# Turning attention weights on VectorE and through DRAM in place of TensorE transposes

## The chip, the cores and the metric

One core of one Trainium2 chip. The metric is the time of the program on the device in microseconds (us). Each time below is the median of some executions of one kernel; figures from a profile are those of one profiled execution. All executions quoted here fell in the fast state, within 1.5% of the fastest of the same kernel. The "granted clock" is TensorE's, as a share of full speed. A matmul of fp32 data leaves two records in the trace, a transpose one. "PE" is TensorE's matmul pipe, "DVE" VectorE, "ACT" ScalarE, "POOL" GpSimd, and "SPq" the sequencer that issues the DMAs.

## The reference

Eight batches of eight heads, 576 positions, 64 values per head. Attention keeps only scores within `tau` of the row's maximum; a feed-forward block with ELU follows. All of it is fp32.

```python
scores = scale * np.matmul(q, k.transpose(0, 1, 3, 2))       # (8, 8, 576, 576)
thresh = np.max(scores, axis=-1, keepdims=True) - tau
scores = np.where(scores >= thresh, scores, -1000000000.0)
attn = np.exp(scores - np.max(scores, axis=-1, keepdims=True))
attn = attn / (np.sum(attn, axis=-1, keepdims=True) + 1e-09)
x = merge_heads(np.matmul(attn, v))                           # (4608, 512)
h = x @ w_in                                                  # (4608, 2048)
g = np.where(h > 0.0, h, np.exp(np.minimum(h, 0.0)) - 1.0)
out = g @ w_out                                               # (4608, 512)
```

## The kernel before

Heads are worked on in 32 pairs, four pairs to a batch. A pair has five steps: four of 128 query positions and a tail step for the last 64 positions of both heads. In a step, `begin` multiplies scores and takes maxima and exponentials, `finish` forms the kept and normalised weights `w`, and one step later `turn` turns `w`, because the product with `v` needs the key position on the partition axis. When two steps (part a) or the last three (part b) of a pair are turned, `values` multiplies.

```python
def finish(pr, i, hs):
    ...
    for h in hs:                                   # DVE: w = (sc >= th) * e, sum beside it
        nc.vector.scalar_tensor_tensor(w[:, h], sc[:, :, :HALF], st["th"][:, h : h + 1], e, ALU.is_ge, ALU.mult, ...)
    ...
    for h in hs:                                   # POOL: w = w / sum
        nc.gpsimd.tensor_scalar(w[:, h], w[:, h], rs[:, h : h + 1], 1.0, ALU.mult, ALU.mult)

def turn(pr, i):
    w = open_steps.pop((pr, i))["w"].rearrange("p h a n -> p (h a n)")
    ...
    for h in range(2):
        rt = ps_t.tile([P, NC, P], FP32, name="rt", tag="rt")
        for c in range(NC):                        # PE: 128x128 transposes into PSUM
            k0 = h * (S + TAIL) + c * P
            transpose(rt[:, c], w[:, k0 : k0 + P])
        nc.scalar.copy(wT[:, h * NC : (h + 1) * NC, cs], rt)     # ACT: PSUM to SBUF
    ...                                            # one more for the last 64 keys of both heads

# the loop from the second batch on; the feed-forward work of the batch before fills TensorE
for n in range(per_seq, len(steps) + 2):
    if n < len(steps):
        ahead(*steps[n])                           # turns q and k, loads two pairs ahead
        begin(*steps[n], [0, 1] if steps[n][1] < NC else [0])
        ...
        finish(*steps[n], [0, 1] if steps[n][1] < NC else [0])
    if n - 1 < len(steps):
        turn(*steps[n - 1])
    behind(*steps[n - 2])                          # values, two steps behind
    due = min(due + rate, len(units))
    while due >= 1 and units:                      # 1.7 units of four matmuls per step
        f, a = units.popleft(); f(*a); due -= 1
```

The order in this loop is not the order on the chip: the compiler schedules each engine's instructions within the dependencies.

## Time and profile before

| | before |
|---|---|
| time, median of 4 in the comparison with the changed kernel | 1615.38 us (1613.23 to 1628.98) |
| period of a group (four pairs and one batch of feed-forward work) | 178.6 us |
| PE busy, whole run | 97% |
| mean granted clock | 0.989 |

The lines on which the prediction rests are shown in the prediction.

### The profile page before, as it was taken

The numbers are of one execution on the slowest core, as the hardware profiler recorded it, in microseconds if no ns is written. First come the engines' busy times: TensorE is split into PE (matmuls) and PEld (weight loads), VectorE is DVE, ScalarE is ACT, GpSimd is POOL, SyncE is SP. The second block draws the span as 40 slices with busy tenths as digits, with TensorE's granted clock in tenths as the row PEclk, the third lists the DMA queues.
The fourth block names the chain that finished last, engine by engine and source line by source line (L and its number), as shares of the span: only waits on it lengthen the run. The fifth ranks groups of instructions, "written<-read, shape, count | busy, mean of one in ns | idle before, by whom it ended". The sixth has DMA issues, their size and how long they took to land.

```text
span 1611.8 us, 17586 instructions
## 1 busy us (share of the span) xinstructions
PE 1570.4 (97%) x5952; PEld 786.4 (49%) x5952; DVE 735.0 (46%) x1670; ACT 586.1 (36%) x1109; POOL 379.6 (24%) x779
## 2 busy tenths in 40 slices
PE   7899889999999999999999999999999999999998
PEld 4554444554454445544555544554555454444443
DVE  6778773455335543455335543455345533220210
ACT  4665653343334433344334433344234333110110
POOL 4654552221222212222122212212122222000000
PEclk8999999999999999999999999999999999999999
DMA  5334541111111101110111011111110000000000
GB/s 108 69 81 104 142 130 36 32 19 23 29 29 29 23 15 36 36 23 15 30 35 30 15 25 27 34 23 23 28 34 10 9 7 14 7 1 20 7 7 20
DMA packets 200553, 55.68 MB, mean 35 GB/s; under 512 B 191760, under 2 KB 191760, under 8 KB 200464
## 3 DMA queue, kind: packets, MB, share of 16 engines
q1 hardware_dynamic: 200464, 54.56, 15.2%
q8 instruction: 48, 0.79, 0.2%
q14 instruction: 41, 0.34, 0.1%
HBM read 45.09 MB, written 9.44 MB: 34 GB/s over the span
## 4 chain that ended last, share of the span: by engine, by line
PE 82%; DVE 7%; POOL 4%; ACT 2%; issue 2%; DMA 1%; SPq 1%; POOLq 0%; DVEq 0%; ACTq 0%
PE po L299 30%; PE ph L285 26%; PE sc L197 9%; PE rt L221 8%; PE pv L269 8%; DVE w L213 3%; POOL w L218 2%; PE pv L266 2%; DVE mx L199 1%; ACT e L204 1%; POOL wtop L134 1%; DMA wst<-in_moe_w_out_dram 1%; DVE gt L290 1%; ACT fe L287 1%; DVE fe L288 1%
## 5 line engine op out<-in xcount | busy, mean ns | idle before, releaser
L299 PE MATMUL po<-w_out_sb,gt 128*128 128x512 f32 x1152 | 520.0, 597 | 0.0
L285 PE MATMUL ph<-xt,w_in_sb 128*128 128x512 f32 x1024 | 464.1, 597 | 0.0
L199 DVE TENSOR_REDUCE mx<-sc 128x1 f32<-128x576 f32 x288 | 207.4, 751 | 304.7 <-PE sc L197 304.6
L299 PEld LDWEIGHTS po<-w_out_sb,gt 128*128 128x128 f32 x1152 | 209.7, 191 | 236.5 <-issue 236.0
L218 POOL TENSOR_SCALAR w<-w,rs 128x576 f32<-128x576 f32 x288 | 217.0, 763 | 357.3 <-DVE rs L216 326.8
L213 DVE SCALAR_TENSOR_TENSOR w<-sc,th,e 128x576 f32<-128x576 f32 x288 | 226.5, 815 | 158.5 <-ACT e L204 150.8
L285 PEld LDWEIGHTS ph<-xt,w_in_sb 128*128 128x128 f32 x1024 | 184.7, 190 | 204.0 <-issue 203.0
L204 ACT ACTIVATE e<-sc,nb,keep 128x576 f32<-128x576 f32 x288 | 227.4, 829 | 83.8 <-POOL nb L200 83.5
L221 PE MATMUL rt<-ident,w 128*128 128x128 f32 (+1 forms) x1344 | 211.5, 284 | 17.9 <-POOL w L218 12.0
L221 PEld LDWEIGHTS rt<-ident,w 128*128 128x128 f32 (+1 forms) x1344 | 153.4, 143 | 118.5 <-issue 46.1
L197 PE MATMUL sc<-kT,qT 64*128 64x288 f32 x1024 | 192.9, 439 | 16.6 <-DVE kT L172 8.2
L288 DVE TENSOR_SCALAR fe<-fe 128x512 f32<-128x512 f32 x144 | 63.7, 443 | 315.3 <-ACT fe L287 315.3
L287 ACT ACTIVATE fe<-ph 128x512 f32<-128x512 f32 x144 | 85.9, 596 | 287.8 <-PE ph L285 287.8
L197 PEld LDWEIGHTS sc<-kT,qT 64*128 64x128 f32 x1024 | 107.1, 190 | 127.1 <-issue 84.9
L200 POOL TENSOR_SCALAR nb<-mx,nkeep 128x2 f32<-128x2 f32 (+1 forms) x176 | 52.1, 296 | 480.8 <-DVE mx L199 404.9
L238 ACT COPY wTa<-rt 128x512 f32<-128x512 f32 x128 | 70.9, 587 | 163.1 <-PE rt L221 161.1
L238 ACT COPY wTb<-rt 128x512 f32<-128x512 f32 x128 | 72.2, 584 | 129.3 <-PE rt L221 128.1
L290 DVE SCALAR_TENSOR_TENSOR gt<-ph,fe 128x512 f32<-128x512 f32 x144 | 99.4, 690 | 5.8
L304 ACT COPY ot<-po 128x512 f32<-128x512 f32 x36 | 21.1, 585 | 181.4 <-PE po L299 181.4
L269 PE MATMUL pv<-wTb,vm 128*64 128x320 f32 x512 | 76.0, 439 | 0.0
L269 PE MATMUL pv<-wTa,vm 128*64 128x256 f32 x512 | 63.6, 391 | 0.0
L285 PE MATMUL ph<-xtail,w_in_sb 128*128 128x512 f32 x128 | 55.1, 592 | 0.0
(45 smaller groups left out, 666.7 us busy)
## 6 DMA issues: line engine op xcount, KB each, us to landing
qm<-in_q_dram SPq DMA_DIRECT2D x128, 72.0 KB, 2.6
km<-in_k_dram SPq DMA_DIRECT2D x128, 72.0 KB, 2.5
vm<-in_v_dram SPq DMA_DIRECT2D x64, 128.0 KB, 2.4
wst<-in_moe_w_in_dram SPq DMA_DIRECT2D x16, 512.0 KB, 4.0
wst<-in_moe_w_out_dram SPq DMA_DIRECT2D x16, 512.0 KB, 3.8
out_dram<-ot SPq DMA_DIRECT2D x32, 256.0 KB, 2.0
vd<-in_v_dram SPq DMA_DIRECT2D x64, 16.0 KB, 2.1
out_dram<-ot SPq DMA_DIRECT2D x8, 128.0 KB, 2.3
```

The lines of the kernel that those rows point to most:

```text
L197: nc.tensor.matmul(scs[h][:, a, :HALF], qs[r], kT[r, k0 : k0 + HALF], start=True, stop=True)
L199: nc.vector.tensor_reduce(st["mx"][:, h : h + 1], scs[h][:, :, :HALF], axis=AX.XY, op=ALU.max)
L204: nc.scalar.activation(e, scs[h][:, :, :HALF], AF.Exp, bias=st["nb"][:, h : h + 1], scale=keep)
L213: nc.vector.scalar_tensor_tensor(w[:, h], sc[:, :, :HALF], st["th"][:, h : h + 1], e, ALU.is_ge, ALU.mult, accum_out=sm[:, h : h + 1])
L218: nc.gpsimd.tensor_scalar(w[:, h], w[:, h], rs[:, h : h + 1], 1.0, ALU.mult, ALU.mult)
L221: nc.tensor.matmul(dst, src, ident, is_transpose=True, skip_group_check=True)
L238: nc.scalar.copy(wT[:, h * NC : (h + 1) * NC, cs], rt)
L269: nc.tensor.matmul(pv[h * D : (h + 1) * D, :n], vm[:, h, c], wT[:, h * NC + c], start=False, stop=(c == NC - 1), skip_group_check=True)
L285: nc.tensor.matmul(ph, w_in_sb[:, j, ft * P : (ft + 1) * P], xt[:, j], start=(j == 0), stop=(j == KJ - 1))
L287: nc.scalar.activation(e, ph, AF.Exp)
L290: nc.vector.scalar_tensor_tensor(gt, ph, 0.0, e, ALU.max, ALU.add)
L299: nc.tensor.matmul(po[:, :DM], gts[ft][:, it * P : (it + 1) * P], w_out_sb[:, ft], start=(ft == 0), stop=(ft == NFT - 1))
```

## The change

From the eighth pair on (25 of 32 pairs, 125 steps), DVE turns `w` in 32x32 squares inside each partition quarter. The squares must still change quarters: four DMAs write the result to DRAM and one reads it back in the right order. TensorE loses 42 transposes per pair, ScalarE the copies behind them.

```diff
+    SWITCH = NPAIR + 3
...
+        if pr >= SWITCH:
+            x = late["x"].tile([P, NT * 2 * GK], FP32, name="x")
+            nc.vector.transpose(x, w)
+            there = dram.tile([NT, T, NT, 2 * GK], FP32, name="there")
+            for p in range(NT):
+                nc.sync.dma_start(there[:, :, p].rearrange("c k n -> k c n"),
+                                  x[p * T : (p + 1) * T].rearrange("k (c n) -> k c n", c=NT))
+            back = there.rearrange("c k p n -> (c k) p n")
+            if i < NC:
+                nc.sync.dma_start(wT[:, g0 : g0 + NT].rearrange("p g c n -> p g (c n)"), back)
+            else: ...                              # the tail step's two outer parts of wTb
+            return
...
-    for n in range(per_seq, len(steps) + 2):
+    for n in range(per_seq, len(steps) + 3):
...
-        behind(*steps[n - 2])
+            turned.append(steps[n - 1])
+        if len(turned) > (2 if late and n < len(steps) else 1) or n >= len(steps):
+            behind(*turned.popleft())              # values three steps behind
```

Cut here: a new layout of `w` and `wT` (keys in another order, so `v` is loaded in 16 small pieces per pair in place of 4), two memsets of `w` in a tail step, products of part b with 384 columns in place of 320 for the first of them, loads one step later, and weight staging buffers that are given back at the switch.

More of the change, by code (lines that the diff above doesn't have):

```diff
@@ L38 @@
     HALF = S // 2
+    T = 32
+    NT = P // T
+    GK = S // NT
+    NCH = 2 * NC + 1
     KJ = DM // P
@@ L44 @@
     FAR = 3.0e37
-    T = 32
+    SWITCH = NPAIR + 3
     assert (D, DM, TAIL * 2, B * TAIL, KJ) == (64, H * D, P, MAIN, NPAIR)
@@ L54 @@
     xpool = ctx.enter_context(tc.tile_pool(name="xpool", bufs=2))
-    wstage = ctx.enter_context(tc.tile_pool(name="wstage", bufs=2))
     gpool = ctx.enter_context(tc.tile_pool(name="gpool", bufs=NFT + 1))
     epool = ctx.enter_context(tc.tile_pool(name="epool", bufs=2))
+    dram = ctx.enter_context(tc.tile_pool(name="dram", bufs=4, space=bass.MemoryType.DRAM))
+    early = ExitStack()
+    wstage = early.enter_context(tc.tile_pool(name="wstage", bufs=2))
+    late = {}
     ps_t = ctx.enter_context(tc.tile_pool(name="ps_t", bufs=2, space=PSUM))
@@ L129, in convert_w @@
         nc.vector.scalar_tensor_tensor(top, hi, 0xC0000000, top, ALU.bitwise_and, ALU.bitwise_or)
-        rest = wstage.tile([P, WN], I32, name="wrest", bufs=1)
+        rest = lo.bitcast(I32)
         nc.scalar.mul(rest, lo, 2.0**-29)
@@ L158, in load @@
         vd = vds[pr % NVD]
+        if SWITCH <= pr < SWITCH + NVD:
+            nc.gpsimd.memset(vd, 0.0)
         for i in range(2):
-            vh = v[b, 2 * j + i]
-            nc.sync.dma_start(vm[:, i], vh[:MAIN].rearrange("(c p) d -> p c d", p=P))
-            r = slice(i * TAIL, (i + 1) * TAIL)
-            nc.sync.dma_start(vd[r, r], vh[MAIN:])
+            if pr < SWITCH:
+                r = slice(i * TAIL, (i + 1) * TAIL)
+                nc.sync.dma_start(vm[:, i], v[b, 2 * j + i, :MAIN].rearrange("(c p) d -> p c d", p=P))
+                nc.sync.dma_start(vd[r, r], v[b, 2 * j + i, MAIN:])
+                continue
+            for g in range(NT):
+                vg = v[b, 2 * j + i, g * GK : (g + 1) * GK]
+                m0, x0, r0 = (0, P, T * g) if i == 0 else (GK - P, 0, T * g + GK - P)
+                nc.sync.dma_start(vm[T * g : T * (g + 1), i], vg[m0 : m0 + P].rearrange("(c t) d -> t c d", t=T))
+                nc.sync.dma_start(vd[r0 : r0 + GK - P, i * D : (i + 1) * D], vg[x0 : x0 + GK - P])
         raws[pr] = *tiles, vm, vd
@@ L172, in prep @@
             nc.vector.transpose(dst, src.rearrange("p j d -> p (j d)"))
-        nc.gpsimd.tensor_copy(kT[D:, :TAIL], kT[D:, S:])
+        if pr < SWITCH:
+            nc.gpsimd.tensor_copy(kT[D:, :TAIL], kT[D:, S:])
         qd = qds[pr % NQD]
@@ L186, in begin @@
             open_steps[pr, i] = {
-                "w": att.tile([P, 2, 2, HALF], FP32, name="w"),
+                "w": att.tile([P, 2 * S], FP32, name="w"),
                 **{x: small.tile([P, 2], FP32, name=x) for x in ("mx", "nb", "th", "sm", "rs")},
@@ L194, in begin @@
             for h in hs:
-                k0 = a * HALF + (0 if h else TAIL)
+                k0 = a * HALF + (0 if h and pr < SWITCH else TAIL)
                 r, qs = (slice(h * D, (h + 1) * D), qT[:, i * P : (i + 1) * P]) if i < NC else (slice(0, P), qd)
@@ L210, in finish @@
         w, sm, rs = st["w"], st["sm"], st["rs"]
+        wg = w.rearrange("p (a g h n) -> p a g h n", a=2, h=2, n=GK)
+        if pr < SWITCH:
+            parts = [(slice(0, P), h, w[:, h * S : (h + 1) * S].rearrange("p (a g n) -> p a g n", a=2, n=GK)) for h in hs]
+        elif i < NC:
+            parts = [(slice(0, P), h, wg[:, :, :, h]) for h in hs]
+        else:
+            parts = [(slice(h * TAIL, (h + 1) * TAIL), 0, wg[h * TAIL : (h + 1) * TAIL, :, :, h]) for h in range(2)]
+            for h in range(2):
+                nc.gpsimd.memset(wg[h * TAIL : (h + 1) * TAIL, :, :, 1 - h], 0.0)
+        for r, s, wv in parts:
+            sc, e = st[s]
+            sc = sc[r, :, :HALF].rearrange("p a (g n) -> p a g n", n=GK)
+            nc.vector.scalar_tensor_tensor(wv, sc, st["th"][r, s : s + 1], e[r].rearrange("p a (g n) -> p a g n", n=GK),
+                                           ALU.is_ge, ALU.mult, accum_out=sm[r, s : s + 1])
         for h in hs:
-            sc, e = st.pop(h)
-            nc.vector.scalar_tensor_tensor(w[:, h], sc[:, :, :HALF], st["th"][:, h : h + 1], e, ALU.is_ge, ALU.mult,
-                                           accum_out=sm[:, h : h + 1])
+            st.pop(h)
         nc.vector.tensor_scalar(sm[:, cs], sm[:, cs], 1e-9, None, ALU.add)
         nc.vector.reciprocal(rs[:, cs], sm[:, cs])
-        for h in hs:
-            nc.gpsimd.tensor_scalar(w[:, h], w[:, h], rs[:, h : h + 1], 1.0, ALU.mult, ALU.mult)
+        for r, s, wv in parts:
+            nc.gpsimd.tensor_scalar(wv, wv, rs[r, s : s + 1], 1.0, ALU.mult, ALU.mult)
     def transpose(dst, src):
@@ L223, in turn @@
     def turn(pr, i):
-        w = open_steps.pop((pr, i))["w"].rearrange("p h a n -> p (h a n)")
+        w = open_steps.pop((pr, i))["w"]
         if i == 0:
-            wTs[pr, 0] = wtp.tile([P, 2 * NC + 1, 2 * P], FP32, name="wTa")
+            wTs[pr, 0] = wtp.tile([P, 2 * NT, NCH, T], FP32, name="wTa")
         if i == 2:
-            wTs[pr, 1] = wtp.tile([P, 2 * NC + 1, 2 * P + TAIL], FP32, name="wTb")
+            wTs[pr, 1] = wtp.tile([P, 3 * NT, NCH, T], FP32, name="wTb")
         wT = wTs[pr, min(i // 2, 1)]
-        n0 = i % 2 * P if i < NC else 2 * P
+        g0 = i % 2 * NT + (NT // 2 if i >= 2 else 0)
@@ new lines, in turn @@
+        if pr >= SWITCH:
[3 more added lines that the diff above has]
+            for p in range(NT):
+                nc.sync.dma_start(
+                    there[:, :, p].rearrange("c k n -> k c n"),
+                    x[p * T : (p + 1) * T].rearrange("k (c n) -> k c n", c=NT),
+                )
+            back = there.rearrange("c k p n -> (c k) p n")
+            if i < NC:
+                nc.sync.dma_start(wT[:, g0 : g0 + NT].rearrange("p g c n -> p g (c n)"), back)
+            else:
+                nc.sync.dma_start(
+                    wT.rearrange("p (a b) c n -> p a b (c n)", b=2)[:, ::5],
+                    back.rearrange("k (a b) n -> k a b n", b=2),
+                )
+            return
@@ L231, in turn, with to @@
+        def to(gs, cs, src, r=slice(0, P)):
+            nc.scalar.copy(wT[r, gs, cs].rearrange("p g c n -> p c g n"), src.rearrange("p c (g n) -> p c g n", n=T))
         if i < NC:
-            cs = slice(n0, n0 + P)
-            for h in range(2):
+            for c0, c1 in ((0, NC), (NC + 1, NCH), (NC, NC + 1)):
                 rt = ps_t.tile([P, NC, P], FP32, name="rt", tag="rt")
-                for c in range(NC):
-                    k0 = h * (S + TAIL) + c * P
-                    transpose(rt[:, c], w[:, k0 : k0 + P])
-                nc.scalar.copy(wT[:, h * NC : (h + 1) * NC, cs], rt)
@@ L239, in turn @@
-            rt = ps_t.tile([P, NC, P], FP32, name="rt", tag="rt")
-            transpose(rt[:, 0], w[:, MAIN : MAIN + P])
-            nc.scalar.copy(wT[:, 2 * NC, cs], rt[:, 0])
+                for c in range(c0, c1):
+                    transpose(rt[:, c - c0], w[:, c * P : (c + 1) * P])
+                to(slice(g0, g0 + NT), slice(c0, c1), rt[:, : c1 - c0])
         else:
+            ga, gb = slice(0, 2), slice(3 * NT - 2, 3 * NT)
             rt = ps_t.tile([P, NC, P], FP32, name="rt", tag="rt")
@@ L246, in turn @@
                 transpose(rt[:, c], w[:, c * P : (c + 1) * P])
-            nc.scalar.copy(
-                wT[:, : 2 * NC, n0:].rearrange("p (h c) n -> p h c n", h=2),
-                rt.rearrange("p c (h n) -> p h c n", h=2),
-            )
+            to(ga, slice(0, NC), rt[:, :, :TAIL])
+            to(gb, slice(NC + 1, NCH), rt[:, :, TAIL:])
             rt = ps_t.tile([P, NC, P], FP32, name="rt", tag="rt")
@@ L253, in turn @@
             transpose(rt[:, 1], w[:, S - P : S])
-            for h in range(2):
-                r = slice(h * TAIL, (h + 1) * TAIL)
-                nc.scalar.copy(wT[r, 2 * NC, n0:], rt[r, h, r])
+            cs = slice(NC, NC + 1)
+            to(ga, cs, rt[:TAIL, :1, :TAIL], slice(0, TAIL))
+            to(ga, cs, rt[TAIL:, 1:2, :TAIL], slice(TAIL, P))
+            to(gb, cs, rt[:, 1:2, TAIL:])
     def values(pr, part):
@@ L263, in values @@
             xts[b] = xpool.tile([P, KJ, MAIN], FP32, name="xt")
-        n = wT.shape[2]
+        n = wT.shape[1] * T
         pv = ps_t.tile([P, 512], FP32, name="pv", tag="rt")
-        nc.tensor.matmul(pv[:, :n], vd, wT[:, 2 * NC], start=True, stop=False, skip_group_check=True)
+        nc.tensor.matmul(pv[:, :n], vd, wT[:, :, NC], start=True, stop=False, skip_group_check=True)
         for c in range(NC):
             for h in range(2):
-                nc.tensor.matmul(pv[h * D : (h + 1) * D, :n], vm[:, h, c], wT[:, h * NC + c],
+                g0, g1 = (2 * h, 2 * h + 10) if part else (0, 2 * NT)
+                nc.tensor.matmul(pv[h * D : (h + 1) * D, g0 * T : g1 * T], vm[:, h, c], wT[:, g0:g1, h * (NC + 1) + c],
                                  start=False, stop=(c == NC - 1), skip_group_check=True)
-        nc.scalar.copy(xts[b][:, j, part * 2 * P : (part + 1) * 2 * P], pv[:, : 2 * P])
+        q0 = TAIL * part
+        nc.scalar.copy(xts[b][:, j, part * 2 * P : (part + 1) * 2 * P], pv[:, q0 : q0 + 2 * P])
         if part:
-            nc.scalar.copy(xtail[:, j, b * TAIL : (b + 1) * TAIL], pv[:, 2 * P : n])
+            for h in range(2):
+                r = slice(h * D, (h + 1) * D)
+                nc.scalar.copy(xtail[r, j, b * TAIL : (b + 1) * TAIL], pv[r, h * (n - TAIL) : h * (n - TAIL) + TAIL])
             pairs.pop(pr)
@@ L325, in ahead @@
             prep(pr + 1)
-            if pr + 2 < NP:
-                load(pr + 2)
+        if i == 3 and pr + 2 < NP:
+            load(pr + 2)
     def behind(pr, i):
@@ L360 @@
         psum[name] = ctx.enter_context(tc.tile_pool(name=f"ps_{name}", bufs=bufs, space=PSUM))
-    while len(turned) > 1:
-        behind(*turned.popleft())
     due = 0.0
     rate = (NFT + NIT * NFT // 4) / (per_seq - 1)
-    for n in range(per_seq, len(steps) + 2):
+    for n in range(per_seq, len(steps) + 3):
         if n < len(steps):
-            ahead(*steps[n])
-            begin(*steps[n], [0, 1] if steps[n][1] < NC else [0])
-            convert_w()
-            convert_w()
-            finish(*steps[n], [0, 1] if steps[n][1] < NC else [0])
-        if n - 1 < len(steps):
+            pr, i = steps[n]
+            hs = [0, 1] if i < NC else [0]
+            ahead(pr, i)
+            begin(pr, i, hs)
+            if not late:
+                convert_w()
+                convert_w()
+            finish(pr, i, hs)
+        if n < len(steps) + 1:
+            if steps[n - 1] == (SWITCH, 0):
+                while turned:
+                    behind(*turned.popleft())
+                assert progress[1] == len(pieces)
+                early.close()
+                late["x"] = ctx.enter_context(tc.tile_pool(name="late", bufs=2))
             turn(*steps[n - 1])
-        behind(*steps[n - 2])
+            turned.append(steps[n - 1])
+        if len(turned) > (2 if late and n < len(steps) else 1) or n >= len(steps):
+            behind(*turned.popleft())
         due = min(due + rate, len(units))
```

## The prediction

> **What bounds the kernel now.** I read the page's busy shares, its slices, its chain and its groups, then the stretches of 100 us and the timeline of one steady step. Page, parts 1, 2 and 4:
>
> ```profile
> PE 1570.4 (97%) x5952; PEld 786.4 (49%) x5952; DVE 735.0 (46%) x1670; ACT 586.1 (36%) x1109; POOL 379.6 (24%) x779
> ...
> PE   7899889999999999999999999999999999999998
> ...
> PE 82%; DVE 7%; POOL 4%; ACT 2%; issue 2%; DMA 1%; SPq 1%; POOLq 0%; DVEq 0%; ACTq 0%
> ```
>
> PE is busy without a hole from about 250 us on and carries 82% of the chain. Everything else hides beside it. The groups that matter:
>
> ```profile
> L221 PE MATMUL rt<-ident,w 128*128 128x128 f32 (+1 forms) x1344 | 211.5, 284 | 17.9 <-POOL w L218 12.0
> ...
> L172 DVE STREAM_TRANSPOSE kT<-km 128x576 f32<-128x576 f32 x32 | 24.6, 769 | 1.1 <-DMA km<-in_k_dram 1.1
> ```
>
> The transposes to be removed are 42 per pair; the mean of 284 ns overlaps with neighbours, so 211.5/1344 = 157 ns each counts. VectorE already turns 128x576 in 769 ns. In the list of longest chain pieces the same PE piece recurs at 683.75 and 862.34 us, so **four pairs (one batch, one group) take 178.6 us**, 44.65 per pair. From the timeline of a late step:
>
> ```profile
> 1362.84 1.24 PE L197 MATMUL sc<-kT,qT 64*128 64x288 f32 x8
> ...
> 1364.11 1.42 DVE L199 TENSOR_REDUCE mx<-sc 128x1 f32<-128x576 f32 x2 [4.39 <-PE sc L197]
> ...
> 1365.70 0.27 POOL L200 TENSOR_SCALAR nb<-mx,nkeep 128x2 f32<-128x2 f32 x1 [4.32 <-DVE mx L199]
> ...
> 1366.00 1.55 ACT L204 ACTIVATE e<-sc,nb,keep 128x576 f32<-128x576 f32 x2 [0.22 <-POOL nb L200]
> ...
> 1366.93 0.82 DVE L213 SCALAR_TENSOR_TENSOR w<-sc,th,e 128x576 f32<-128x576 f32 x1 [1.40 <-ACT e L204]
> ```
>
> This is the softmax loop of one step. Scores start at 1362.84, the second w ends 0.82 + 0.74 after 1366.93, near 1368.5: 5.65 us. The two score buffers are then free. PE hides this loop only because each step has some 8 feed-forward matmuls to issue meanwhile.
>
> **What the Trainium skill says.** "VectorE: DVE Perf Modes", section The three transpose paths: VectorE turns 32x32 blocks only, never a whole 128x128. So the quarters must travel; the trace has the first half (769 ns), not yet the journey. "DMA: Bandwidth & Descriptors", section Anatomy of one DMA: some 2 us of a DMA are fixed, mostly the write's receipt; the trace agrees (256 KB of out_dram land in 2.0 us, 72 KB of km in 2.5). "TensorE: Matmul & The Clock Gate", section Part 2: weight loads are pulled ahead, but matmuls "stay in program order". I rest most on this one: in the timeline PE runs exactly the compiled order of its matmuls. Same page, Why this matters for your kernels: gaps over about 3 us halve the clock. The trace agrees in kind: PE waits 1.96 us before the values at 102.72, and the clock granted from 104 to 106 is 0.56.
>
> **The change part by part.**
>
> *Removed from PE.* From pair 7, 25 pairs x 42 = 1050 transposes. What the steady group holds apart from them: 128 feed-forward matmuls (each two records) at 0.861 us = 110.2; scores per pair 4 x 1.17 + 0.97 = 5.65 (868.28 to the next group's start at 869.45; 879.89 to 880.86); values 2.43 + 2.93 = 5.36 (871.35 to 873.78; 1384.13 to 1387.06). That is 110.2 + 4 x 11.0 = 154.2, so transposes with their switches cost 178.6 - 154.2 = 24.4 per group, 6.1 per pair: 25 x 6.1 = **152 us off PE**. ACT loses its copies too, off the path.
>
> *Added to VectorE.* One 128x1152 transpose per step, an estimate of 1152/576 x 0.6 + 0.17 = 1.37 us; 125 of them are 171 us. Each stands, in the compiled order, between mx and w of the next step, where the trace has a hole of 1.40 us. Alone, this is nearly free. A tail step costs a second w of 0.8.
>
> *Added to the DMA queue.* Per step 4 writes and 1 read, 1.2 MB: at 7.7 us a step, 154 GB/s. A 4-us window of before (16 to 20) moves 288. Issue, at 0.3 to 0.5 us each as in the trace: per pair 8 q/k, 16 v, 20 + 5 others, about 22 us. Below a pair's time, but the 24 loads stand between the writes of two steps, so an x buffer can come free late: 24 loads at 0.48 are 11.5, the writes and reads before and the writes after them some 5, landings 2 x 2.5: about 21 us, where two sparse steps and a tail give 16 to 20.
>
> *Moved, and this decides.* The compiler's scheduler fixes PE's order. Before, each full step carries 4 to 8 feed-forward matmuls. In the changed kernel one steady group reads, with letters of mine for its twenty steps (sc scores, q those of the tail step, ph and po feed-forward, PVa and PVb the nine value products of a pair's first and second part):
>
> ```
> A sc4 ph27 | B sc4 ph8 | C sc4 ph5 po3 | D q2 PVb | E sc2 po6 sc2 po8
> F sc2 PVa sc2 po34 | G sc4 po8 | H sc4 po5 | I q2 | J sc1 PVb sc3
> K sc1 PVa sc3 ph1 | L sc4 ph1 | M sc4 | N q1 PVb q1 | O sc2 ph4 sc2
> P sc1 PVa sc3 | Q sc4 | R sc4 | S q1 PVb q1 ph2 | T sc2 ph12 PVa sc2 ph4
> ```
>
> Ten steps, I to R, hold 6 feed-forward matmuls together; A and F alone hold 61. In I to R PE has nothing to hide the softmax behind.
>
> Walk from the end of H's last w to the end of S's scores (X: the new transpose of the step before):
> - a full step without filling: mx 1.42, X 1.4 in the hole, two w 1.56, then 1.07 until the next scores are in: 5.45. L, M, Q, R: 21.8.
> - I: q 1.1, half of J's scores, PVb 3.04 and the other half 3.6, J's mx 0.75 (it stands ahead of I's w), X 1.4, w 1.6: 8.45.
> - J, O: X must wait until POOL has scaled the tail's weights, 2.0 after their w; then X 1.4, w 1.65 and 0.1 of hand-over: 5.15 each.
> - K, P: scores with PVa 2.43 inside end 2.85 after the last w; mx 1.42, q and k turned 1.54, X 1.4, w 1.6: 8.8 each.
> - N: q with PVb inside ends 3.25 after the last w; mx 0.76, X 1.4, O's first mx 0.75, w 1.65: 7.8.
> - S: its q with PVb inside: 3.25.
>
> Sum **69.2 us**. PE's work in it: scores 3 x 0.97 + 8 x 1.17 = 12.3, values 3 x 3.04 + 2 x 2.43 = 14.0 (PVb is 2.93 plus 0.11, as its first product grows from 320 to 384 columns), six ph 5.2: 31.5. So PE idles 37.7. The rest of the group is PE-bound: 122 feed-forward matmuls 105.0, scores 10.3, values 7.9: 123.2. Group: 192.4 before any other stall. I add, as estimates, 8 for x buffers that come free late behind the loads (two or three times a group, 2 to 5 each) and 5 for the halved clock in the sparse stretch: 205.4 against 178.6, so **+27 per group** instead of -24.
>
> Sum: 1617, five such groups (pairs 11 to 30) +135; pairs 7 to 10, where the order is still mostly even: -24 + 7 = -17; the last pair (I to N once more, 20 idle, then the last weights go softmax, turn, DRAM and back, 10 more, minus 6): +24; wider copies and later loads in the first pairs: +6. **1765 us.**
>
> **The rivals.**
>
> *1. The plain gain.* If PE were filled evenly, 1617 - 152 plus some 10 at the end: 1475. For it: 97% busy PE, VectorE at 46%, a hole that fits X. Against it: PE follows its compiled order, and that is sparse in ten of twenty steps.
>
> *2. The transfers become the bound.* 1152-byte packets, DRAM written and read; had each step to wait for its own round trip (about 9 us from X to landing), values would stall PE. Against it: the scheduler places values two to five steps behind, so the weights have landed. Then only VectorE's wait for an x buffer is left, within my 8 us. If it were 20 per group: 1820.
>
> *3. Sparse stretch, but mild.* If the inserted values cost less than I count and no x buffer is late, idle falls to 30 per group: 154 + 30 and 2 for switches = 186, and the sum about 1670.
>
> *4. The clock.* With gaps of some 4 us in every sparse step the clock may be halved all through I to S: scores +0.9 a step, each value block +2.5: some 20 more per group, 1840.
>
> **Range and chances.** From rival 4 down to just above rival 3, as it asks for two things at once: 1690 to 1840. Within 2% (1585 to 1650) would need the sparse steps, stalls and all, to take under 60 us, where VectorE's own work (mx, w, X, q and k turned, some 25 a pair) already fills 51 and every step has a hand-over to PE and back. Faster needs the compiled order not to bind. I give 0.04 to each.
>
> **What will show it.** PE's busy share falls from 97% to about 80%, with slices at 9 alternating with slices at 4 to 5, period some 205 us. The chain of waits shows DVE (mx, x, w) at 20% or more. DVE's x transposes: 125, near 1.4 us. PE's waits: sc behind DVE w, tens of us in all. rt drops to 294 records. Wrong if PE stays at 9 through (rival 1), if pv waits on DMA (rival 2), or if the dense stretches take more than 122 us.

## More of the kernel before

One more view is useful for comparing: the busy times of the engines within one group (columns: stretch, its length, busy us and instructions of each engine, granted clock, DMA share, GB/s).

```profile
868.28:1046.88 178.60, 178.10 (x715) 89.80 (x714) 82.61 (x188) 66.73 (x128) 39.56 (x88) 1.00 0.13 26
```

PE is busy for 178.10 of 178.60 us at full clock, while DVE works less than half of the time and the DMA engines are 13% busy. Work taken off PE should shorten this, if nothing else takes PE's place.

## The result, and the profile after

The changed kernel takes 1840.33 us (1831.25 to 1843.46, four runs) against 1615.38 us. The ratio is 1.1363, with a 95% interval of 1.1288 to 1.1438. Ratios in this document are the mean time of one kernel's fast runs over the mean of the other's fast runs of the same rounds, so not quite the ratio of the medians. The profiled run (1839.97 us) has a mean clock of 0.903.

The page of the changed kernel, parts 1, 2 and 4:

```profile
PE 1611.9 (88%) x4902; PEld 749.1 (41%) x4902; DVE 918.8 (50%) x1845; ACT 444.4 (24%) x780; POOL 427.1 (23%) x832
...
PE   7988899899769996799868996699966998589999
...
PEclk8999999999769997799868997699977998799999
DMA  4434434443673537634475426736376343500001
...
PE 63%; DMA 10%; SPq 9%; DVE 9%; issue 4%; POOL 3%; ACT 2%; DVEq 0%; POOLq 0%; ACTq 0%
```

Slices of 9 alternate with slices of 6 and 7, and the granted clock falls in the same slices, in which DMA is busiest. PE's busy time did not fall by 152 us but rose from 1570.4 to 1611.9: matmuls that ran slower took more than the removed transposes had. Two of the groups:

```profile
L270 DVE STREAM_TRANSPOSE x<-w 128x1152 f32<-128x1152 f32 x125 | 170.6, 1365 | 7.9 <-POOL w L252 5.0 <-DMA there<-x 2.9
...
L217 PE MATMUL sc<-kT,qT 64*128 64x288 f32 x1024 | 282.9, 506 | 116.6 <-DVE w L245 104.8 <-DVE kT L191 8.0 <-DMA vm<-in_v_dram 3.1
```

The new turn costs what was predicted, and it waits for a free buffer (`there<-x`) 2.9 us in the whole run. PE's scores wait for DVE's weights, hardly for DMA. One group, in three stretches with the columns named above:

```profile
866.30:899.00 32.70, 32.70 (x89) 14.53 (x87) 9.97 (x19) 3.69 (x6) 4.24 (x10) 1.00 0.22 62
899.00:987.00 88.00, 57.92 (x180) 27.34 (x180) 51.24 (x99) 19.62 (x34) 24.54 (x51) 0.69 0.70 182
987.00:1082.00 95.00, 95.00 (x280) 43.58 (x279) 51.14 (x99) 20.88 (x34) 17.69 (x36) 1.00 0.43 108
```

A group lasts 215.0 us (853.47 to 1068.42 by the same long piece of feed-forward work). In 88 us of it PE is busy for 57.92 at a clock of 0.69, in the rest it is full. Two steps from the middle of the sparse stretch, in the timeline of PE and DVE:

```profile
963.42 3.02 PE L217 MATMUL sc<-kT,qT 64*128 64x288 f32 x8 [4.61 <-DVE w L245]
...
965.74 1.50 DVE L219 TENSOR_REDUCE mx<-sc 128x1 f32<-128x576 f32 x2 [1.23 <-PE sc L217]
967.15 1.37 DVE L270 STREAM_TRANSPOSE x<-w 128x1152 f32<-128x1152 f32 x1
...
968.66 0.82 DVE L245 SCALAR_TENSOR_TENSOR w<-sc,th,e 128x576 f32<-128x576 f32 x1
...
969.40 0.81 DVE L245 SCALAR_TENSOR_TENSOR w<-sc,th,e 128x576 f32<-128x576 f32 x1
...
969.54 3.02 PE L217 MATMUL sc<-kT,qT 64*128 64x288 f32 x8 [3.10 <-DVE w L245]
```

PE multiplies scores, then has nothing to do until DVE has worked through maxima, the turn and the weights: 6.12 us a step, with gaps of 3.10 and 4.61 us. The same eight records of score products that took 1.24 us before take 3.02. The granted clock is 0.50 in both bursts, so the four records of one head take 2.28 us against 1.23; the other head's start 0.74 us later, when DVE's second `w` has freed their buffer.

### The profile page after: what moved, and what is told of

It is laid out like the page before. It is cut to its first block, busy times and chain, and to the rows that moved or that the text cites. A ratio compares the mean times of both kernels' runs of the same rounds, so it can differ in the third digit from the quotient of the medians.

```text
span 1838.2 us, 16656 instructions
## 1 busy us (share of the span) xinstructions
PE 1611.9 (88%) x4902; PEld 749.1 (41%) x4902; DVE 918.8 (50%) x1845; ACT 444.4 (24%) x780; POOL 427.1 (23%) x832
## 4 chain that ended last, share of the span: by engine, by line
PE 63%; DMA 10%; SPq 9%; DVE 9%; issue 4%; POOL 3%; ACT 2%; DVEq 0%; POOLq 0%; ACTq 0%
PE po L358 24%; PE ph L344 22%; PE sc L217 9%; DMA there<-x 9%; PE pv L325 5%; SPq L160 3%; SPq L273 2%; DVE w L245 2%; DVE mx L219 2%; SPq L182 2%; DVE x L270 2%; SPq L181 2%; PE pv L321 2%; ACT e L224 1%; POOL wtop L142 1%
## 5 line engine op out<-in xcount | busy, mean ns | idle before, releaser
L217 PE MATMUL sc<-kT,qT 64*128 64x288 f32 x1024 | 282.9, 506 | 116.6 <-DVE w L245 104.8
L252 POOL TENSOR_SCALAR w<-w,rs 128x576 f32<-128x576 f32 x313 | 238.1, 770 | 479.4 <-DVE rs L250 471.9
L358 PEld LDWEIGHTS po<-w_out_sb,gt 128*128 128x128 f32 x1152 | 215.1, 190 | 269.7 <-issue 269.5
L245 DVE SCALAR_TENSOR_TENSOR w<-sc,th,e 128x576 f32<-128x576 f32 x313 | 246.7, 814 | 46.5 <-ACT e L224 23.1
L217 PEld LDWEIGHTS sc<-kT,qT 64*128 64x128 f32 x1024 | 151.1, 217 | 259.0 <-DVE w L245 122.8
L220 POOL TENSOR_SCALAR nb<-mx,nkeep 128x2 f32<-128x2 f32 (+1 forms) x176 | 54.6, 310 | 541.0 <-DVE mx L219 490.5
L270 DVE STREAM_TRANSPOSE x<-w 128x1152 f32<-128x1152 f32 x125 | 170.6, 1365 | 7.9 <-POOL w L252 5.0
L325 PE MATMUL pv<-wTb,vm 128*64 128x320 f32 x512 | 92.2, 512 | 0.0
L217 PE MATMUL sc<-kT,qd 128*128 128x288 f32 x128 | 48.5, 490 | 39.0 <-DVE w L245 32.9
L328 ACT COPY xt<-pv 128x256 f32<-128x256 f32 x64 | 23.8, 372 | 224.2 <-PE pv L325 224.2
L255 PE MATMUL rt<-ident,w 128*128 128x128 f32 (+1 forms) x294 | 51.9, 304 | 15.7 <-POOL w L252 12.2
L325 PEld LDWEIGHTS pv<-wTb,vm 128*64 128x64 f32 x512 | 40.1, 163 | 58.5 <-issue 42.0
```

What stands on the lines that cost most here:

```text
L217: nc.tensor.matmul(scs[h][:, a, :HALF], qs[r], kT[r, k0 : k0 + HALF], start=True, stop=True)
L245: nc.vector.scalar_tensor_tensor(wv, sc, st["th"][r, s : s + 1], e[r].rearrange("p a (g n) -> p a g n", n=GK), ALU.is_ge, ALU.mult, accum_ ...
L252: nc.gpsimd.tensor_scalar(wv, wv, rs[r, s : s + 1], 1.0, ALU.mult, ALU.mult)
L270: nc.vector.transpose(x, w)
L325: nc.tensor.matmul(pv[h * D : (h + 1) * D, g0 * T : g1 * T], vm[:, h, c], wT[:, g0:g1, h * (NC + 1) + c], start=False, stop=(c == NC - 1), ...
L358: nc.tensor.matmul(po[:, :DM], gts[ft][:, it * P : (it + 1) * P], w_out_sb[:, ft], start=(ft == 0), stop=(ft == NFT - 1))
```

## The experiments

The first four, then e5 to e7, e8 and e9, and e10 to e12: each set shared runs of the kernel before, whose medians were 1612.7, 1623.0, 1612.6 and 1612.6 us. Every run has three rounds.

| run | result | time, us | ratio to before | group, us | clock |
|---|---|---|---|---|---|
| e1_pin | correct | 1840.44 | 1.1376 | 215.1 | 0.910 |
| e2_nodma | wrong | 1546.92 | 0.9552 | 165 to 168 | 0.991 |
| e3_pinfast | correct | 1847.32 | 1.1419 | 213 to 215 | 0.896 |
| e4_nodmafast | wrong | 1741.45 | 1.0753 | 196.7 | 0.919 |
| e5_never | correct | 1639.93 | 1.0128 | 180.9 | 0.984 |
| e6_order | correct | 1622.78 | 1.0024 | 177.5 | 0.955 |
| e7_idletrip | wrong | 1712.97 | 1.0572 | 191 to 195 | 0.936 |
| e8_all_order | correct | 1516.82 | 0.9385 | 160.8 | 0.984 |
| e9_all_idletrip | wrong | 1524.98 | 0.9429 | 160.8 | 0.975 |
| e10_values_first | correct | 1558.30 | 0.9657 | 167.2 | 0.982 |
| e11_queue_free | correct | 1538.96 | 0.9519 | 161 to 164 | 0.979 |
| e12_order_no_dram | correct | 1639.94 | 1.0154 | 179.5 | 0.986 |

### e1 to e4: sparse steps or the way through DRAM?

The theory was the prediction's: the loss is PE's compiled order, bunched feed-forward work and sparse steps, while the transfers are hidden. The rival: the transfers cost the time. Two switches make four runs. e1 ties PE to the order of the program, in which every step carries four or eight feed-forward matmuls; the call puts an instruction behind the one emitted before it on its engine:

```diff
+    def mm(*a, **k):
+        ins = nc.tensor.matmul(*a, **k)
+        if pinned:                                 # set where the feed-forward loop starts
+            tc.keep_in_program_order(ins)
...
-                nc.tensor.matmul(scs[h][:, a, :HALF], ...)      # and so for every matmul
+                mm(scs[h][:, a, :HALF], ...)
```

> The changed kernel, with every TensorE matmul from the second batch on pinned to the order of the program, so that each step carries 4 to 8 feed-forward matmuls again; transposes, transfers and results are unchanged. If the uneven order of TensorE is the cause (my theory), the loss is gone and the removal shows: 1617 less 152 plus some 10 to 20 at the end and for early pairs, so 1475 to 1510, TensorE busy over 96%, clock over 0.98. If the transfers through DRAM or the queue that issues them are the bound, it stays above 1750.

e2 takes the trip away and lets DVE write into the tiles that PE reads; without it the compiled order came out even by itself.

```diff
-            nc.vector.transpose(x, w)              # and four writes and the read-back
+                nc.vector.transpose(wT[:, g0 : g0 + NT].rearrange("p g c n -> p (g c n)"), w)
```

> The changed kernel with the trip through DRAM taken out: VectorE turns the squares straight into the buffers that TensorE reads (wrong result on purpose). Nothing is pinned; the compiled order of TensorE comes out even by itself. Theory of the uneven order: 1460 to 1500, within 1% of e1. Theory of the transfers: also fast, so this run tells only together with e1: if e1 is much slower than this one, the transfers cost time by themselves.

e3 is e1 with the feed-forward work issued faster than even, so that about ten of a group's twenty steps hold none; e4 is the same without the trip.

```diff
-        due = min(due + rate, len(units))
+        due = min(due + (rate if not late else rate * 19 / 11), len(units))
```

> e1 with one number changed: from the late part on, the feed-forward units of a batch are dealt out at 32 in 11 steps instead of 32 in 19, so that some 9 or 10 steps of 20 carry none, in pinned order. Transfers unchanged. Theory of the uneven order with the halved clock: the loss comes back, by 30 to 50 us a group in six groups: 1680 to 1800, TensorE clock in the sparse steps near 0.6. If bunching is harmless and something else in the changed kernel was slow: as e1.

> e3 without the trip through DRAM (wrong result on purpose): sparse steps, but no transfer and no buffer that waits for one. Theory of the uneven order: within 30 of e3 (I put late buffers at 8 a group). Theory of the transfers, which the chain of waits of the changed kernel suggests with its 10% for DMA and 9% for the queue: near e2, below 1520.

Measured: 1547 us even without the trip, 1741 bunched without it, 1840 even with it, 1847 bunched with it. e1 missed my theory's range and fell where the rival has it, above 1750. The other three missed their ranges: e2 lies 47 us above 1500, e3 47 above 1800, and e4 in between what the two theories expect of it. So both causes are real, and they do not add. Sparse steps alone, without the trip, cost 195 us (e4 against e2). This is the cost of e4's bunching, nine empty steps in a row, which is not quite the changed kernel's. e4 is pinned and e2 is not, but in the trace PE of e2 has the same four or eight feed-forward matmuls in every step as in e1 from the switch on, so the pin is not what parts them. But an even order with the trip is no better than the changed kernel: **e1 refutes the view that the order of the matmuls is the only cause**. In e1 the waits of PE are others:

```profile
PE pv L204 <- DMA wTb<-there: 118.9, 16, 8.4
PE sc L204 <- DVE w L252: 66.4, 30, 4.4
PE pv L204 <- DMA there<-x: 55.6, 7, 9.2
```

and in the changed kernel they were

```profile
PE sc L217 <- DVE w L245: 137.6, 47, 4.6
...
PE pv L321 <- DMA wTb<-there: 12.9, 1, 12.9
```

(Columns: what waited for what, us in total, times, longest.) In the changed kernel PE's value products waited for a read-back once, for 12.9 us, in the last pair. In e1 they wait 174.5 us for the trip. The timeline of e1 shows why the trip is so long; these are the weights of one tail step:

```profile
894.97 15.93 SPq L280 DMA_DIRECT2D there<-x  x4
...
896.82 1.56 POOL L259 TENSOR_SCALAR w<-w,rs 64x576 f32<-64x576 f32 x2 [2.23 <-DVE rs L257]
...
909.19 1.37 DVE L277 STREAM_TRANSPOSE x<-w 128x1152 f32<-128x1152 f32 x1
...
911.05 0.34 SPq L286 DMA_DIRECT2D wTb<-there  x1
...
917.42 1.37 DVE L277 STREAM_TRANSPOSE x<-w 128x1152 f32<-128x1152 f32 x1
...
919.60 0.53 SPq L288 DMA_DIRECT2D wTb<-there  x1
...
925.21 1.62 PE L204 MATMUL pv<-wTb,vd 128*128 128x384 f32 x2 [9.15 <-DMA there<-x]
```

The tail's weights are ready at 898.38 (896.82 + 1.56). Their turn starts only at 909.19: DVE has done a whole other step first. Their read-back is issued at 919.60, because in the queue it stands behind the first write of the next step, which waits for that step's turn at 917.42. From ready weights to the read-back's issue it takes 21.2 us. The four writes "of 15.93 us" are the same thing seen from the queue: three belong to the step before, the fourth waits for the late turn, and the read-back at 911.05 stands behind it. The Trainium skill has this in "DMA: Bandwidth & Descriptors", section Anatomy of one DMA — SWDGE (gpsimd) path: the DMA engines do not wait on semaphores, any such wait happens on the issuing sequencer before dispatch. The section is on DMAs that GpSimd issues; here SyncE issues, and the trace agrees: nothing was issued between 894.97 and 910.90 but these four.

The same is in the changed kernel. In its compiled order of DVE, 119 of the 125 turns stand one full step later than they could, behind the next step's weights; in e1 68 do.

### e5: the other edits

The switch to the new way is never reached; everything else of the change stays.

```diff
-    SWITCH = NPAIR + 3
+    SWITCH = 99
...
+    if not late:
+        early.close()                          # the early buffers, else given back at the switch
```

> The changed kernel with the switch never reached: TensorE transposes all through, but the new weight layout, 384-column tail products, later loads and copies of the change stay. If these side edits carry part of the loss, this run is slower than the kernel before by tens of us; if they cost only what was worked out (2 to 8 us in all), it takes 1610 to 1640 us.

1639.93 us, 1.3% over before (interval 1.0069 to 1.0187), at the upper edge of the expectation. The side edits cost some 20 us in this form, not 2 to 8. In the traces 16 us of it lie before the second batch's first output copy (442.59 against 426.12 us), and each later group takes 180.9 us in place of 178.6. Which edit costs it was not followed up: most of the 227 us is elsewhere.

### e6 and e7: the order of the queue and of the turn

The new theory: the trip is not too slow, its parts are issued too late. e6 is e1 with the order of the DMAs fixed (a step's writes, up to seven of the loads, its own read-back, then the next step), with the turn fixed right behind the next step's maxima, and with the value products after the step's feed-forward work.

```diff
+    def pin(ins):
+        if late: tc.keep_in_program_order(ins)
...
-            finish(pr, i, hs)
+            if not late:
+                finish(pr, i, hs)
...
             turn(*steps[n - 1])
...
+            if was and n < len(steps):
+                finish(pr, i, hs)                  # now behind the turn of the step before
...
-            nc.vector.transpose(x, w)
+            pin(nc.vector.transpose(x, w))         # so too the maxima and the weights
...
+            load_some(7)                           # loads between the writes and the read-back
-        if len(turned) > (2 if ...) ...: behind(*turned.popleft())
         while due >= 1 and units: ...
+        if len(turned) > (2 if ...) ...: behind(*turned.popleft())
```

> Correct kernel. TensorE even and in program order as in the first experiment, and now the queue too: a step's four writes, up to seven of the next pair's loads, then its own read-back, before the next step's writes; the VectorE turn always right behind the next step's maxima; the value products of a step three steps behind, after that step's feed-forward work. Theory A (the way through DRAM is only too long because the read-back stands behind the next step's first write and the turn comes late): a read-back is then landed about 11 to 12 us after its turn, values wait little, and the time is 1480 to 1580. Theory B (the queue or the transfers themselves cannot pass a step in 7.7 us): values still wait for DMA by some 150 us in all, and the time stays above 1750. In between, 1600 to 1750: part of each.

e7 has the same orders and transfers, but nobody waits for them: DVE writes straight into PE's tiles, the DMAs carry those to DRAM and back into a spare tile.

> Wrong result on purpose. The same orders as e6_order, with the same writes, read-backs and loads, but VectorE turns straight into the tiles that TensorE reads, and the read-back lands in a spare tile that nobody reads. Theory A: TensorE waits for nothing of DMA, 1470 to 1560, and the distance to e6_order is the cost of the wait alone. Theory B (throughput of the queue, or contention that slows other work): well above 1600, as VectorE must wait until the writes have read the tiles.

e6 takes 1622.78 us, 218 us less than e1 with the same work and the same even order of PE. PE waits for no DMA any more. That is short of theory A's 1480 to 1580: it fell between the two theories, "part of each". What was left is a wait of 72.7 us for `w`. The timeline of DVE in e6:

```profile
903.32 1.49 DVE L245 TENSOR_REDUCE mx<-sc 128x1 f32<-128x576 f32 x2 [0.77 <-PE sc L161]
...
909.62 0.43 DVE L374 TENSOR_SCALAR fe<-fe 128x512 f32<-128x512 f32 x1 [4.81 <-ACT fe L373]
...
913.51 0.69 DVE L376 SCALAR_TENSOR_TENSOR gt<-ph,fe 128x512 f32<-128x512 f32 x1
914.12 1.37 DVE L296 STREAM_TRANSPOSE x<-w 128x1152 f32<-128x1152 f32 x1
...
915.41 0.78 DVE L271 SCALAR_TENSOR_TENSOR w<-sc,th,e 128x576 f32<-128x576 f32 x1
```

Between maxima and turn stand two feed-forward operations that wait for this step's own matmuls. DVE is idle for 4.81 us with a turn and weights ready to be done.

e7 came out at 1712.97 us, 90 us slower than e6, which neither theory had. DVE's `w` waits 97.9 us for ACT's exponentials, against 17.9 in e6: in one step the bias of an exponential was ready at 911.1 us, but the exponential ran at 916.1, behind an output copy and two copies of values. The compiled order of ACT had changed with the edit, so this run says nothing on the transfers.

### e8 and e9: every engine in order

e8 adds the rest of DVE, ACT and POOL to the pinned order from the switch on, and puts the turns of q and k behind the weights of their step. e9 is the same with the trip that nobody reads.

```diff
+    class InOrder:                                 # wraps an engine, pins each call
+        def __init__(self, engine): self.engine = engine
+        def __getattr__(self, op):
+            return lambda *a, **k: pin(getattr(self.engine, op)(*a, **k))
+    VEC, ACT, POOL = InOrder(nc.vector), InOrder(nc.scalar), InOrder(nc.gpsimd)
```

> Correct kernel: e6_order with ScalarE and GpSimd and the rest of VectorE's work in program order too in the late part, and the q and k turns behind the weights of their step. In e6 the feed-forward's fe and gt had been let in ahead of the turn and the weights, and PE still waited 73 us for w. Theory A (what was left in e6 is the order of the softmax chain, not the transfers): PE's wait for w falls under 20 us, values do not wait for DMA, and the time is 1480 to 1560, below both kernels. Theory B (contention of the transfers with the engines, or the queue): it stays within 30 us of e6, 1590 to 1650.

> Wrong result on purpose: the same orders as e8_all_order, with the trip through DRAM made but read by nobody. e7_idletrip came out slower than e6_order, and there ScalarE stood for 5 us with an output copy ahead of an exponential that was ready; if that order was the cause, this run is now at or below e8_all_order, and the distance is what the wait for the trip still costs: 0 to 30 us under theory A. If contention alone costs time, both lie well above 1547, the time without transfers.

e8 takes **1516.82 us**, correct, 6% faster than the kernel before and 323 us faster than the changed kernel. It is the version that beats both. Its page:

```profile
PE 1467.7 (97%) x4902; PEld 691.9 (46%) x4902; DVE 915.2 (60%) x1845; ACT 446.2 (29%) x780; POOL 425.1 (28%) x832
...
PE   7987989999999999999999999999999999999998
...
PEclk9986999999999999999999999999999999999999
DMA  5423541376666766676667666766667655000000
```

The same 4902 PE records as in the changed kernel, with PE full and the clock up. PE waits for no DMA, and for DVE's `w` 10.7 us in the run. A tail step in its timeline, to set beside that of e1:

```profile
1031.57 1.66 POOL L163 TENSOR_SCALAR w<-w,rs 64x576 f32<-64x576 f32 x2 [1.76 <-DVE rs L163]
...
1033.44 1.42 DVE L163 TENSOR_REDUCE mx<-sc 128x1 f32<-128x576 f32 x2 [0.91 <-PE sc L171]
...
1034.78 1.37 DVE L163 STREAM_TRANSPOSE x<-w 128x1152 f32<-128x1152 f32 x1
...
1036.17 1.94 SPq L168 DMA_DIRECT2D there<-x  x4
...
1042.07 0.53 SPq L168 DMA_DIRECT2D wTb<-there  x1
```

The weights are ready at 1033.23, turned from 1034.78, and read back from 1042.07: 8.8 us in place of 21.2.

e9 takes 1524.98 us. The same transfers that nobody waits for cost the same as those that PE depends on, so **in e8 the wait for the trip costs nothing that can be seen**. What contention by the transfers costs is not isolated, as no run has e8's orders without them. Nothing points to it: PE is busy for 159.62 of a group's 160.77 us, and a weight operation of DVE takes 814 ns in e8 and 815 before, an exponential of ACT 829 in both. Both runs lie below e2's 1547; e2's DVE had waited 152.7 us for POOL's scaling, as turns stood right behind the weights that they turn.

### e10 to e12: one part undone at a time

e10 moves the value products back ahead of the feed-forward work. e11 takes the pins off the DMAs and emits a pair's 24 loads in one step again. e12 keeps TensorE's transposes all through, with the pinned orders of e8; it also places the last of a step's three groups of transposes behind the step's feed-forward work (not shown).

```diff
# e10: the two blocks of e6's last edit swapped back
# e11
-        pin(nc.sync.dma_start(dst, src))
+        nc.sync.dma_start(dst, src)
-                loads.append(load_gen(pr + 2))     # seven per step
+                load(pr + 2)                       # all at once
# e12
-    SWITCH = NPAIR + 3
+    SWITCH, ORDER = 99, NPAIR + 3                  # pins start at ORDER, the new way never
```

> Correct kernel: e8_all_order with one part undone, the value products of three steps back placed right behind the scores, ahead of the step's feed-forward work, as in e1_pin. From e8's trace: a turn starts 2.7 us behind its step's scores, its read-back lands some 11.7 us later, 14.4 in all, and the products would start 16 us behind those scores. If that holds, nothing waits and the time is 1515 to 1550; if the place of the products was what cured e1_pin, values wait for DMA by over 60 us in all and it takes over 1580.

> Correct kernel: e8_all_order with another part undone, the queue: the order of the DMAs is the compiler's again and a pair's 24 loads are emitted in one step, as in the changed kernel. In the compiled order read-backs stand behind up to four writes of the next step, and the 24 loads (some 11 us of issue) stand between the writes of two steps. If the queue's order was the main cause of e1_pin's waits, values wait for DMA and VectorE's turn for its buffer, by 60 to 250 us in all: 1580 to 1800. If it was not, 1515 to 1550.

> Control, correct kernel: TensorE transposes all through (the switch never reached), but the orders of e8_all_order on every engine from the eighth pair on. If e8's gain over the kernel before is the transposes removed from a full TensorE, this run is near e5_never, 1600 to 1650; if it is the pinned order itself, it comes down towards 1520 to 1560.

e10: 1558.30 us, 41 more than e8; the waits for read-backs are 12.7 us, not over 60. Neither of the two outcomes, but nearer the first. e11: 1538.96 us, 22 more; DVE's turn waits 34.0 us for a buffer and PE's products 6.2 us for a read-back:

```profile
PE pv L171 <- DMA wTb<-there: 12.7, 7, 2.4
...
DVE x L163 <- DMA there<-x: 34.0, 15, 4.3
```

(The first line is of e10, the second of e11.) **The queue's order, which I had taken for the main cause in e1, is a small one** once the turn is on time. In e11 the read-backs stand behind a write of the next step again, and by the times of issue and landing a trip is as long as in e1: from the start of the turn to the landing of its read-back the median is 16.1 us, 14.7 in e1 and 11.3 in e8. What e11 still has and e1 lacks is the order of DVE, ACT and POOL, with 124 of 125 turns on time, and the later place of the values. e12: 1639.94 us, the same as e5, so pinning gains nothing by itself. The gain of e8 comes from the transposes removed: 123 us between e12 and e8.

## Why the prediction was right, and where its steps were off

The verdict held, and so did the place of the loss: 88 us of a group of 215 in which PE has almost no feed-forward work behind which to hide the softmax. e4 against e2 shows that such steps can cost 195 us without the trip. What did not hold is that this is the only cause: e1, with every step filled, is as slow. The median of 1840.33 us lies a third of a microsecond above the stated range and 75 us above the figure. That the fourth rival names 1840 is in part luck: it has 42 us more per group, where 36.5 were measured, and 24 for the last pair, where the table has 51.

To see which terms were mis-sized, both runs are cut where PE starts the first score product of a pair: pair 7 at 264.5 us before and 264.4 after, pair 11 at 443.1 and 465.4, pair 31 at 1336.0 and 1542.7, the end at 1611.8 and 1838.2. At these cuts the two kernels have not done the same share of the feed-forward work: 184, 440 and 1720 of its 2304 matmul records before, 168, 498 and 1792 after. The last column takes this lead out at 0.43 us a record, half of the prediction's 0.861 us; it is an estimate.

| stretch | predicted | measured | without the lead |
|---|---|---|---|
| pairs 0 to 6 | +6 | -0.1 | +6.8 |
| pairs 7 to 10 | -17 | +22.4 | -9.4 |
| pairs 11 to 30, five groups | +135 | +184.4 | +178.4 |
| pair 31 and the end | +24 | +19.7 | +50.7 |

- **"Pairs 7 to 10, where the order is still mostly even"** was about right. The first sparse stretch, from 470 to 560 us with the clock at 0.77, 0.72 and 0.66 in three stretches of 30 us, begins behind the tail step of pair 10 and belongs to the first of the five groups.
- **The five groups** are 43 of the 79 us by which the sums of this table differ. **The walk of 69.2 us with 8 for late buffers and 5 for the clock**, 82.2 together, takes 88.0. Late buffers are nearly nothing (2.9 us in the run). PE is busy for 57.9 us, where the walk had 31.5, and idle for 30.1, where it had 37.7. By subtraction the clock costs about 19 a group, not 5, the term that the fourth rival put at 20. A bound from the trace fits: the clock was 0.50 for 54.6 of the 88 us, PE was busy for 37.15 of these, and at full clock it would have saved at most half of that, 18.6. It was not isolated by a run.
- **The rest of a group at 123.2** takes 127.0, above the bound of 122 that I set as a sign of error; 3.8 us a group.
- **The last pair at +24** is 27 of the 79 us. From 1542.7 to 1620 us PE is idle for 33.5, close to the 20 and 10 expected, with 12.9 for the last read-back in it. But the clock is 0.66 to 0.78 meanwhile, and the term had nothing for that; how its rest divides is not shown.
- **152 us off PE** was somewhat too much: e12 to e8 gives 123.
- **"The scheduler places values two to five steps behind, so the weights have landed"** holds in the changed kernel (one wait of 12.9 us). But it led to a wrong inference, which the first rival states: that PE "filled evenly" would give 1475. e1 has it filled evenly and takes 1840. The bunched order and the long trip are exchangeable: with the values late PE runs out of other work, with the values early PE waits for them. I missed it by taking each turn to stand "in the compiled order, between mx and w of the next step": there stands a turn, but in 119 of 125 cases that of an older step. For the same reason the waits of the turn for POOL, which the walk counted in J and O, hardly came: 5.0 us in the run.

Of the signs: the turn's 1.4 us, the 294 remaining transposes and scores waiting for DVE's `w` (137.6 us) were right. PE at 80% was wrong (88%), as slow matmuls count as busy, and with it the slices of 4 to 5. DVE at 20% of the chain was wrong (9%): the chain runs over SPq and DMA for 19%. Taken by itself, the chain would have pointed at the transfers. It is no measure of what they cost: e8, with the same transfers, has 2% on SPq and 2% on DMA; e4, without the trip, still loses 7.5%; and e11, at 1539 us, has more of both than the changed kernel:

```profile
PE 49%; DMA 19%; SPq 18%; DVE 5%; issue 4%; POOL 3%; ACT 2%; DVEq 0%; POOLq 0%; ACTq 0%
```

What stays open: how the 260 us or so between e1 and e8 that e10 and e11 do not account for (323 - 41 - 22) divide between the turn on time, the rest of DVE's order, ACT's and POOL's. These were only undone together, and the parts need not add: no run has the values of e10 and the queue of e11 at once, where each may take away the slack that hid the other. From e6 to e8 it is 106 us for the feed-forward operations on DVE, the q and k turns, ACT and POOL. Why the compiler bunched the order is not shown either; only that it does not, once the trip is taken out (e2).

## What to carry to other kernels

Work taken off a full engine is worth its time only if the engine's order stays even: read the compiled order per step, then ask for each step what hides the serial chain. Where a result travels through DRAM, follow one item from ready to landed in the timeline, and put its producer and its DMAs in order before judging the transfer: here the same trip and the same work took 1840 us or 1517. An experiment that takes away one suspected cause may show no gain because another takes its place at once, as e1 did; only runs with both taken away tell.

## What the Trainium skill lacked or had wrong

- "TensorE: Matmul & The Clock Gate", section Why this matters for your kernels, warns of gaps over some 3 us. The runs agree for such gaps: behind those of 4.61 and 3.10 us the granted clock was 0.50. But in the kernel before it fell to 0.50 from 104.24 to 107.66 us after a wait of only 1.96 us, with PE busy for 2.04 of the 4 us from 100 to 104. So a shorter gap can be enough, and what the prediction calls agreement in kind does not confirm the 3 us.
- Same page, section Part 4: PE-mode transpose, gives some 275 ns for one of bf16 in a kernel's context. The trace's mean of 284 ns, for fp32, is near it, but that is a duration in the pipeline; 1050 transposes taken out at equal order (e12 to e8) gave 123 us, 117 ns each, with their copies' effects. The page has no figure for this.
- "DMA: Bandwidth & Descriptors", section Anatomy of one DMA — SWDGE (gpsimd) path, puts the fixed part of a DMA at some 2 us, for DMAs that GpSimd issues. Here SyncE issues, and a write of 144 KB to DRAM landed in a median of 2.9 us in e8 and 4.1 us in the changed kernel, the same bytes more bunched. No page has a figure for writing a tile to DRAM and reading it back in another order: in e8 it took 8.7 to 13.9 us, in the median 11.3, from the start of the turn to the landing of the read-back.
- No page says how much the order of issue alone can decide: 323 us of 1840 between the changed kernel and e8.
